# A new written-out order of pieces from the 560th on, and a one-column exponential ahead of softmax exponentials, in a fused attention and token-mixing kernel

## Chip, core and metric

One Trainium2 chip, one of its cores. The metric is device time in microseconds (us). TensorE (PE; its weight loads are PEld), VectorE (DVE), ScalarE (ACT) and GpSimd (POOL) each work through one queue of instructions in order; SyncE (SP) issues the transfers. PE's results stand in PSUM banks, which DVE and ACT read.

## What is computed

Eight batches of 576 tokens. Attention with keys and values pooled by eight, then a token and channel mix with a data-dependent rotation:

```
k_p, v_p = mean of k, v over 8 tokens
attn = softmax(scale * q @ k_p^T) @ v_p               # 8 heads of 64
x = heads side by side                                # 8 x 576 x 512
theta = x @ w_theta
zr, zi = x * cos(theta), x * sin(theta)
u = x + w_tok_r @ zr + w_tok_i @ zi
out = u + max(u @ w_ch, 0)
```

## The kernel before

Matrix products run in three terms (high times high, high times low, low times high) so that each factor is split into a rounded high part and a low rest. The work of a batch `b` is cut into streams, each a Python generator, and each step of a generator up to its `yield` is one piece. The names of the streams are the letters in the schedule:

- `k`, `K`, `Q`, `v`, `V` load and pool keys and values and load queries of a batch.
- `S b.m` (`soften`, one of five tiles of queries): scores on PE (tile `s`, or `s_av` and `s_px`), row maximum (L761), subtraction into `e_eps` (L778), the exponential on ACT (L782), sum, reciprocal (L784, L786), division into `en` (L789, L796), and a transposition into `G`.
- `E` and `X` (`turn`, `attend`): the weights times the values, into the banks `pv_av`, `pv_px`, `pv_s`; copies to `xa` or `xb` follow.
- `Y` and `y` turn `x` through DRAM into `xt`.
- `T b.m` (`rotate`, `theta`): 12 matmuls into the one bank `pt` (L932); ACT rounds it into `g` (L936); DVE subtracts it from `pt` (L938), and with that the bank is free; ACT takes the sine of `g` (L983), ACT or DVE its absolute value (L946, L948), ACT the cosine (L987, a sine with an offset). DVE or POOL multiply both into `z` (L990, L992). The tiles `g` and `sn` have one buffer each.
- `Z b.c` (`take`): a cast of a chunk of `z` into `zh` and the rest into `zl`.
- `M b.c.h` (`mix`): 27 matmuls into a bank `py` of 256 or 320 columns (L1038), DVE adds them to `x` (L1044), and the sum is split into `uh` and `ul`.
- `F b.c.h` (`final`): 12 matmuls into a bank `pf` (L1066), DVE adds the positive part (L1071), transposes (L1077), and four transfers write the output. `py` and `pf` share two banks.

What sets the order is a table of 2131 words. Each word names a stream and runs its next piece; a last letter `v`, `g` or `a` is the engine (DVE, POOL, ACT) for a piece that can be put on several:

```python
    for word in SCHEDULE.split():
        name, engine = (word[:-1], word[-1]) if word[-1] in "vga" else (word, None)
        now[0] = engine
        next(streams[name])
```

So the order of the words is the order of the instructions on each engine. ACT holds one set of function tables at a time: sine and exponential are in different sets, and the compiler puts an ACT_TABLE_LOAD ahead of an activation whose set isn't there. Copies and casts by all engines stand under the helper's line L206 (ACT) or L208 (DVE, POOL), and POOL's arithmetic under L191.

Of the kernel before, what the change touches and what calls it, by code (L numbers as in the profile page):

```python
# [58 lines left out]
F0.2.1 S2.3 Z1.0a M1.1.0 M1.1.1 S2.2 M1.1.1 S2.3 M1.1.1 S2.3 Z1.0g M1.0.1 S2.3g F0.2.0 S2.3v F0.3.1 M1.0.1 S2.4 X2.0
S2.4 M1.1.1 X2.0a S2.3 M1.0.1 S2.4 V3.0g K3 X2.0a Y2.0 S2.4g Y2.0 M1.0.0 S2.4g Y2.0 X2.0a M1.0.1 T2.0a M1.0.0 K3a  # L60
T2.0g F0.1.1 Q3.1 F0.3.1 S2.4 Z1.3a Q3.1 M1.0.0 T2.0 T2.0 Z1.3v M1.0.1a K3 K3a M1.0.1g Y2.0 S3.2 T2.0 Y2.0 Z1.2a V3.2v
T2.0 E2.2 S3.2 T2.1a M1.3.1 M1.1.1g M1.0.0 S3.4 S3.3 Z1.2g y2.0 M1.3.0 S3.2 F0.0.1 M1.3.0 T2.0 T2.0 T2.0a S3.2 M1.1.0a
M1.3.0 E2.2 M1.1.1g M1.3.1 S3.2g S3.2v S3.3 T2.0 M1.3.0 M1.2.1 T2.0g T2.1g S3.3 M1.3.1 v3.1 S3.3 F0.1.1 M1.2.1 T2.1
S3.2 S3.3g S3.3v M1.3.1 M1.3.0a S3.4 k4.2 T2.1 X2.2 M1.3.1g F0.0.1 S3.3 V3.1g S3.4 T2.1 M1.2.0 F0.2.1 M1.2.1 S3.4 Y2.2
X2.2a Y2.2 F0.2.1 Y2.2 M1.2.0 X2.2a M1.0.0a S3.4g k4.0 X2.2a T2.2a Y2.2 T2.0v S3.4v S3.0 S3.4 Y2.2 T2.2g u3 M1.2.1
M1.2.1g T2.1 T2.1 S3.0 S3.1 M1.2.0 T2.1 M1.2.1g M1.3.1v V3v F1.3.1 E3.2 T2.1a T2.1 M1.3.0g F1.3.1 M1.2.0 F1.3.1 T2.1v
S3.0 F1.3.1 F1.1.1 y2.2 M1.2.0g M1.2.0g F1.1.1 F1.1.1 T2.1v T2.3a E3.2 S3.0 S3.0v T2.2 F1.3.1 F1.3.1 F1.1.1 T2.2 T2.2
S3.0g F1.0.1 S3.1 T2.4g T2.2 T2.2 F1.2.1 F1.1.1 F1.0.1 M1.1.0v F1.1.1 T2.3v F1.2.1 K4.0g F1.0.1 M1.0.0g F1.0.1 S3.1
T2.3 S3.0 T2.3 S3.1 F1.2.1 F1.2.1 X3.2 T2.3 T2.2 T2.2a k4.1 F1.2.1 T2.2 T2.2g T2.2g T2.3 F1.0.1 F1.0.0 F1.2.0 K4.2g
S3.1g F1.0.0 X3.2a X3.2a X3.2v T2.3 Y3.2 F1.2.0 T2.4a T2.4a T2.4v T2.3 T2.3a F1.2.1 F1.2.0 T2.4 F1.0.1 T2.4 T2.4 T2.3  # L70
T2.3g F1.0.0 Y3.2 Y3.2 T2.3v T2.4 S3.1g F1.2.0 F1.0.0 Q4.0 T2.4 Y3.2 F1.1.0 T2.4 S3.1 K4.1g F1.1.0 T2.4 T2.4v k5.0
T2.4 F1.1.0 T2.4 F1.1.0 T2.4 K4 Z2.1v F1.3.0 F1.2.0 K4a E3.0 F1.3.0 Z2.1v F1.3.0 E3.0 Z2.0a M2.1.0 F1.3.0 M2.1.0 Q4.0
M2.1.0 Z2.0v M2.1.1 M2.1.0 K5.0v M2.1.1 M2.1.1 M2.1.1 M2.1.1g T3.3a M2.0.0 M2.0.1 T2.4 M2.0.1 F1.2.0 M2.1.0v M2.0.1 K4
Z2.2v T2.4 M2.1.1v v4.1 T3.3v Y3.2 F1.1.0 M2.0.1 F1.1.0 v4.2 M2.0.1v X3.0 M2.0.0 M2.0.0 Z2.3v M2.0.0 F1.0.0 Y3.0
F1.3.0 X3.0v X3.0v X3.0v Q4.1 T3.1v Y3.0 Y3.0 T3.1v Z2.2g V4.1g K4a Z2.3v M2.2.1 M2.3.0 M2.2.1 M2.2.1 T3.1 V4.2g
M2.1.0v k5.2 M2.2.1 T3.1 M2.3.0 T3.1 Q4.1 M2.2.1v M2.2.0 S4.0 K5.2g M2.2.0 T3.1 T3.1 M2.2.1g Y3.0 M2.2.0 T3.0a Y3.0
S4.0 v4.0 M2.0.0g M2.3.0 F1.0.0 y3.0 T3.0g T3.0 S4.0 S4.0 S4.0v S4.0g T3.1 M2.3.0 V4.0g S4.1 S4.0 M2.2.0 v5.2 T3.1a
T3.0 T3.0 M2.3.1 M2.3.1 S4.1 T3.1 T3.1v M2.2.0a S4.1 T3.1g T3.0 S4.1 S4.1v T3.0 Q5.0 T3.2a y3.2 S4.1g S4.1 M2.3.1 T3.0
S4.2 T3.3 M2.3.0v M2.2.0g T3.0a T3.2v T3.0 M2.3.1 T3.0v T3.3 F1.3.0 M2.0.0v F2.2.0 T3.0v F2.0.0 T3.3 T3.3 k5.1 K5.1g
M2.3.1a F2.0.0 V4v M2.3.0v F2.0.0 M2.0.1v T3.3 F2.0.0 S4.2 F2.2.0 T3.3 T3.3a F2.0.0 T3.3 F2.2.0 S4.2 E4.0 E4.0 V5.2g  # L80
F2.2.0 M2.3.1v T3.2 T3.3v F2.1.1 T3.2 F2.0.0 T3.3v T3.2 F2.2.1 F2.1.1 F2.1.1 T3.2 S4.2 T3.2 S4.2g F2.2.1 F2.1.1 F2.2.1
S4.3 S4.2v F2.2.1 T3.2 F2.3.1 v5.1 S4.3 F2.0.1 T3.2a T3.2 T3.2g F2.3.1 u4 T3.2g F2.3.1 S4.4 S4.2 Z3.0a S4.3 Z3.1a
F2.2.1 F2.2.0 F2.0.1 F2.0.1 K5 F2.3.1 F2.0.1 Q5.0 S4.3 k6.2 M3.0.0 S4.3v F2.1.0 F2.1.0 Z3.0g S4.3g V5g F2.1.0 M3.0.0
F2.1.0 F2.2.1 F2.1.0 V5.1g S4.4 M3.0.0 F2.2.0 F2.3.0 Q5.1 F2.3.0 F2.3.0 K5a F2.3.0 F2.3.0 K5 X4.0 M3.0.0 S4.3 F2.3.0
X4.0a Y4.0 v5.0 X4.0a M3.0.1 Y4.0 Z3.1v M3.0.1 M3.0.1 M3.1.1 X4.0a S4.4 S4.4 Y4.0 S4.4v Z3.2a T4.0a S4.4v F2.1.0
M3.0.1 T4.1a T4.0g V5.0g M3.1.1 Q5.1 S4.4 T4.0 M3.1.0 M3.1.1 Y4.0 M3.1.0 M3.1.1 K5a S5.2 Z3.2g Y4.0 S5.2 S5.2 M3.1.0
E4.2 M3.0.0a F2.0.1 E4.2 T4.1v Z3.3a M3.1.0 S5.2 S5.3 y4.0 S5.2g T4.0 M3.2.1 S5.2v T4.0 u5 S5.3 M3.2.1 S5.3 T4.0
F2.3.1 M3.3.0 S5.4 T4.0 S5.3 S5.2 Z3.3g S5.3v T4.0 T4.0a M3.3.0 M3.1.1a M3.0.1v M3.2.1 M3.3.0 T4.1 S5.3v M3.0.1v S5.4
T4.0 F2.0.1 F2.1.1 M3.2.1 v6.1 X4.2 S5.4 T4.1 M3.3.1 T4.0g Q6.0 F2.1.1 S5.4 F2.3.1 M3.2.1v T4.1 M3.3.1 S5.3 T4.0g
X4.2a Y4.2 M3.3.0 M3.1.1v M3.2.0 T4.1 Y4.2 M3.1.0g Y4.2 V6.1g M3.3.0g X4.2v S5.4g Y4.2 S5.4g M3.2.0 T4.1 S5.4 X4.2a  # L90
S5.0 M3.2.0 T4.2v K6.2g S5.0 M3.0.0g M3.1.0v T4.2v T4.1 Y4.2 M3.3.1 M3.3.1 S5.1 T4.3v T4.2 M3.3.1a T4.1v T4.2 F3.1.1
M3.2.0 T4.2 k6.0 E5.2 S5.0 M3.2.1v M3.3.1v T4.3g F3.3.1 y4.2 F3.3.1 F3.1.1 F3.1.1 F3.3.1 S5.0 T4.1 M3.2.0a E5.2 S5.0v
S5.0g T4.1g S5.1 F3.3.1 T4.1g F3.1.1 S5.1 F3.0.1 F3.3.1 F3.1.1 S5.1 T4.2 F3.2.1 M3.3.0g F3.2.1 F3.3.1 K6.0g F3.0.1
F3.1.1 F3.2.1 F3.0.1 F3.2.1 T4.2 T4.2 T4.2a T4.2 T4.3 M3.2.0g S5.0 T4.2v F3.0.1 F3.0.1 T4.4a T4.2v T4.3 T4.3 F3.2.1
X5.2 Y5.2 S5.1g X5.2a F3.0.0 F3.1.0 F3.0.0 X5.2a X5.2v F3.1.0 T4.4v T4.3 S5.1g T4.3 F3.0.0 v6.2 T4.3 T4.3a k6.1 F3.0.1
T4.4g T4.3 T4.4v T4.3g T4.3g Y5.2 S5.1 T4.4 Y5.2 F3.1.0 F3.1.0 F3.0.0 F3.2.1 T4.4 T4.4 K6.1g T4.4 F3.2.0 F3.3.0 F3.3.0
T4.4 F3.3.0 F3.2.0 T4.4 T4.4 F3.2.0 K6 F3.3.0 T4.4v Y5.2 E5.0 T4.4 T4.4 K6a T4.4 K6 E5.0 T5.3a Z4.0v F3.0.0 F3.0.0
M4.0.0 M4.0.0 F3.2.0 Z4.0v Z4.1a v6.0 M4.0.0 M4.0.1 M4.0.0 M4.0.1 M4.1.0 Y5.2 M4.1.0 T4.4 V6.2g T4.4 M4.0.1 Z4.2a
# [10 lines left out]
M5.0.0 M5.0.0 S6.3 F4.1.1 S6.3g S6.3g M5.0.0 F4.1.1 M5.0.1 K7 F4.2.1 S6.4 M5.0.0 S6.4 M5.0.1 F4.3.0 X6.0 M5.0.1 K7a
S6.4 Z5.1v M5.1.0 S6.3 S6.4g F4.2.1 M5.1.0 M5.0.1 F4.0.1 X6.0a M5.1.0 S6.4v F4.0.1 F4.3.0 Y6.0 F4.0.1 S6.4 M5.1.0 Y6.0  # L110
M5.1.1 Z5.2a X6.0v M5.1.1 Q7.1 X6.0v F4.1.1 Y6.0 Q7.1 M5.1.1 F4.0.1 M5.1.1 E6.2 S7.2 S7.2 Z5.3a S7.2 Z5.2g Z5.3v
M5.2.1 M5.2.1 S7.3 E6.2 M5.3.1 S7.2 Y6.0 S7.2g M5.0.0g Y6.0 S7.2g M5.2.1 V7.1g M5.0.1v S7.3 F4.0.1 M5.0.1v M5.3.1 X6.2
# [1094 lines left out]
```

## Time and profile before

| what | value |
|---|---|
| median of 3 runs | 594.06 us (590.54, 594.06, 595.79) |
| the profiled execution | 590.58 us, span of its instructions 588.8 us |
| busy: PE, DVE, POOL, ACT | 559.9, 434.6, 306.8, 291.2 us |
| mean granted clock of PE | 0.986 |

Times inside the profile are counted from the first instruction. In a row of the timeline the bracket at the end is the idle time of the engine before the instruction, and what ended it. PE's busy time takes in the modelled ends of pipelined matmuls, so that it says when PE stood still, and not how fast it ran.

### The profile page before, as it was taken

How to read it: one execution, taken by the hardware profiler on the slowest of the kernel's cores; microseconds unless marked ns; L12 is line 12 of the kernel's file. 1: busy time of each engine (PE TensorE's matmuls, PEld its weight loads, DVE VectorE, ACT ScalarE, POOL GpSimd, SP SyncE). 2: the span in 40 equal slices, each digit the busy share in tenths (PEclk: the TensorE clock that was granted, in tenths of full speed). 3: DMA queues.
4: the chain of work that ended last, by engine and by line, in shares of the span. 5: the costliest groups of instructions: out<-in, count | busy, mean ns of one | idle time of the engine just before them, and what ended most of it. 6: DMA issues, size and time to landing. Idle time of an engine off the chain costs nothing.

```text
span 588.8 us, 13209 instructions
## 1 busy us (share of the span) xinstructions
PE 559.9 (95%) x4904; PEld 500.6 (85%) x4904; DVE 434.6 (74%) x857; ACT 291.2 (49%) x589; POOL 306.8 (52%) x445
## 2 busy tenths in 40 slices
...
GB/s 260 269 281 117 117 86 44 122 130 147 97 125 128 164 128 110 163 182 96 132 114 150 165 124 106 191 147 91 80 103 146 68 48 21 90 90 30 13 49 73
DMA packets 191265, 70.63 MB, mean 120 GB/s; under 512 B 149600, under 2 KB 176224, under 8 KB 191200
## 3 DMA queue, kind: packets, MB, share of 16 engines
...
q8 instruction: 39, 0.64, 0.5%
...
HBM read 45.15 MB, written 15.73 MB: 103 GB/s over the span
## 4 chain that ended last, share of the span: by engine, by line
PE 79%; DVE 7%; DMA 4%; POOL 4%; SPq 2%; issue 2%; ACT 2%; POOLq 0%; DVEq 0%; ACTq 0%
PE py L1038 37%; PE pt L932 15%; PE pf L1066 14%; PE s L719 2%; SPq L848 2%; PE pv_av L879 2%; PE pv_av L870 1%; DMA z<-in_v_dram 1%; PE pv_px L870 1%; PE vpp L598 1%; POOL xl L191 1%; PE warm L298 1%; PE s_av L719 1%; PE kpp L598 1%; DMA kprst<-in_k_dram 1%
## 5 line engine op out<-in xcount | busy, mean ns | idle before, releaser
L1038 PE MATMUL py<-WTh,zh 128*128 128x256 f32 (+1 forms) x576 | 87.1, 298 | 2.1 <-DVE zh L208 2.0
L1038 PE MATMUL py<-WTl,zh 128*128 128x256 f32 (+1 forms) x576 | 87.6, 296 | 0.0
L1038 PE MATMUL py<-WTh,zl 128*128 128x320 f32 (+1 forms) x576 | 85.6, 296 | 0.9 <-DVE xb L1044 0.9
L1038 PEld LDWEIGHTS py<-WTh,zh 128*128 128x128 f32 x576 | 80.4, 190 | 4.9 <-DVE zh L208 2.6
L1038 PEld LDWEIGHTS py<-WTl,zh 128*128 128x128 f32 x576 | 80.4, 189 | 1.2 <-issue 0.8
L1038 PEld LDWEIGHTS py<-WTh,zl 128*128 128x128 f32 x576 | 78.9, 188 | 3.0 <-DVE xb L1044 1.3
L191 POOL TENSOR_TENSOR zl<-z,zh 128x384 fp32r<-128x384 f32 (+1 forms) x68 | 53.6, 821 | 29.3 <-ACT zh L206 18.2
L191 POOL TENSOR_TENSOR en<-e_eps,ri 128x256 f32<-128x256 f32 (+3 forms) x66 | 40.3, 630 | 40.4 <-DVE ri L786 27.7
L936 ACT ACTIVATE g<-pt,c_magic 128x512 f32<-128x512 f32 x35 | 24.1, 688 | 57.8 <-PE pt L932 48.2
L932 PE MATMUL pt<-th,xh 128*128 128x512 f32 x148 | 41.9, 405 | 5.3 <-DVE g L938 5.1
L206 ACT CAST zh<-z 128x1152 fp32r<-128x1152 f32 x22 | 25.4, 1152 | 42.8 <-PE py L1038 38.3
L1066 PE MATMUL pf<-uh,chh 128*128 128x256 f32 (+1 forms) x256 | 43.6, 297 | 1.2 <-DVE xb L1071 1.2
L1066 PE MATMUL pf<-ul,chh 128*128 128x256 f32 (+1 forms) x256 | 44.3, 297 | 0.0
L1066 PE MATMUL pf<-uh,chl 128*128 128x256 f32 (+1 forms) x256 | 43.6, 295 | 0.0
L932 PE MATMUL pt<-tl,xh 128*128 128x512 f32 x148 | 41.5, 403 | 0.0
L932 PE MATMUL pt<-th,xl 128*128 128x512 f32 x148 | 41.0, 400 | 0.0
L1066 PEld LDWEIGHTS pf<-uh,chh 128*128 128x128 f32 x256 | 37.5, 188 | 4.0 <-DVE xb L1071 1.8
L1066 PEld LDWEIGHTS pf<-uh,chl 128*128 128x128 f32 x256 | 37.4, 188 | 1.4 <-issue 0.5
L1066 PEld LDWEIGHTS pf<-ul,chh 128*128 128x128 f32 x256 | 37.4, 188 | 1.0
L782 ACT ACTIVATE e_eps<-e_eps 128x576 f32<-128x576 f32 (+1 forms) x30 | 20.6, 687 | 35.4 <-DVE e_eps L778 35.2
L1044 DVE TENSOR_TENSOR xb<-py,xb 128x320 f32<-128x320 f32 x32 | 15.5, 484 | 26.1 <-PE py L1038 25.7
L932 PEld LDWEIGHTS pt<-th,xh 128*128 128x128 f32 x148 | 25.4, 188 | 10.5 <-issue 2.6
...
## 6 DMA issues: line engine op xcount, KB each, us to landing
...
out_dram<-R SPq DMA_DIRECT2D x112, 40.0 KB
out_dram<-R SPq DMA_DIRECT2D x112, 32.0 KB
```

What stands on the lines that cost most here:

```text
L191: nc.gpsimd.tensor_tensor(out[:, r], a[:, r], b[:, r], op)
L206: nc.scalar.copy(out, src)
L598: nc.tensor.matmul(main[:, 2 * j : 2 * j + 2, :], ident, st[:, :, D * r : D * r + D], **steps[r])
L719: nc.tensor.matmul(scs[hh][o : o + 64, SP * c : SP * c + SP], qT[r, c, t0 + o : t0 + o + 64], kpT[r, c, SP * hh : SP * hh + SP], start=Tru ...
L782: nc.scalar.activation(e[:n], e[:n], AF.Exp, scale=scale)
L848: queue.dma_start(Ex[32 * j : 32 * j + 32, 0:m, i], Gx[32 * i : 32 * i + 32, 0:m, j])
L870: nc.tensor.matmul(out(a, y)[half(x_)], Vs[b][half(y), c], weights(half(y), c), start=True, stop=False,)
L932: nc.tensor.matmul(pt, l[:, c, :], r[:, c, :], start=i == 0, stop=i == 11)
L936: nc.scalar.activation(g, pt, AF.Identity, bias=c_magic)
L1038: nc.tensor.matmul(py[:, :n], l[:, kk, :], r[:, kw, t], start=i == 0, stop=i == 3 * NK - 1)
L1044: nc.vector.tensor_tensor(u, py[:, :n], u, ALU.add)
L1066: nc.tensor.matmul(pv[:, :n], l[:, kk, o], uhl[r][:, kk, t], start=i == 0, stop=i == 11)
```

## The change

Counted from 0, words 0 to 559 of the table stay. From the 560th on (while batch 0 is mixed, near 110 us of the profile) the same 1571 pieces stand in another order: a piece moves by 8 places in the mean, the farthest by 131. 149 of them run on another engine: 44 go from DVE to POOL, 33 from POOL to DVE, 27 from DVE to ACT, 17 from ACT to POOL, 16 from POOL to ACT, 12 from ACT to DVE. Counted over the built program, ACT has 39 instructions more (566 for 527), DVE 29 fewer (830 for 859), POOL 11 more; PE and SP have the same instructions in another order. Table loads on ACT are 44 instead of 40. An exponential stands between the sine and the cosine of one `T` piece, with a load before each, five times instead of three times.

The second part is in `soften` and `rotate`: where the last activation was a sine, a one-column exponential of a constant is issued ahead of the softmax exponential, 20 times in all. It waits for nothing, so that the load that the compiler puts before it waits for nothing either.

```diff
+    c_one = const([P, 1], F32, "c_one")
...
+    table = [None]
+    def exp_table():
+        if table[0] != AF.Exp:
+            nc.scalar.activation(c_one, c_eps, AF.Exp)
+            table[0] = AF.Exp
+    def sine(*args, **kw):
+        nc.scalar.activation(*args, AF.Sin, **kw)
+        table[0] = AF.Sin
...
+            exp_table()
             nc.scalar.activation(e[:n], e[:n], AF.Exp, scale=scale)
...
-            nc.scalar.activation(s, g, AF.Sin, scale=-TWO_PI)
+            sine(s, g, scale=-TWO_PI)
...
-M0.0.1a T1.1a k3.0 T1.4 F0.0.0 K3.0g F0.1.0 T1.1 F0.0.1 S2.0 T1.1 T1.1 T1.4 S2.1 F0.2.0 F0.0.0 S2.1 T1.4 Q3.0 T1.4
+M0.0.1a T1.1a k3.0 T1.4 F0.0.0 K3.0g F0.1.0 T1.1 F0.0.1 S2.0 T1.4 T1.3g T1.1 T1.1 F0.0.0 S2.1 T1.4 S2.1 T1.4 F0.2.0
...
```

The added lines move the line numbers by 13 in `soften` (L719 becomes L732) and by 15 from there on (L1038 becomes L1053), and all sines stand under L707, all one-column exponentials under L703.

Place 1, near 254 to 262 us, tiles of batches 2, 3 and 4. PE before, the rows right behind the scores `s4_1`, up to the third theta of batch 3, `pt3_3`:

```order
L932 MATMUL pt3_0_3449<-tl_107,xh3_0_3420 128x512 x4
L932 MATMUL pt3_0_3449<-th_106,xl3_0_3421 128x512 x4
L1038 MATMUL py2_3_1_3500<-WTh_516,zl2_3_3254 128x320 x9
L1038 MATMUL py2_3_1_3500<-WTl_517,zh2_3_3253 128x320 x9
L1038 MATMUL py2_3_1_3500<-WTh_516,zh2_3_3253 128x320 x9
L719 MATMUL s4_2_3566<-kpT_101,qT4_2981 64x72 x16
L932 MATMUL pt3_3_3583<-th_106,xh3_3_3144 128x512 x4
```

PE after, from the same scores to the same theta:

```order
L1053 MATMUL py2_3_0_3307<-WTh_517,zl2_3_3261 128x256 x9
L1053 MATMUL py2_2_0_3383<-WTl_518,zh2_2_3186 128x256 x9
L947 MATMUL pt3_0_3492<-th_107,xh3_0_3376 128x512 x4
L947 MATMUL pt3_0_3492<-tl_108,xh3_0_3376 128x512 x4
L1053 MATMUL py2_2_0_3383<-WTh_517,zl2_2_3187 128x256 x9
L732 MATMUL s4_2_3525<-kpT_102,qT4_2956 64x72 x16
L947 MATMUL pt3_0_3492<-th_107,xl3_0_3377 128x512 x4
L1053 MATMUL py2_3_1_3549<-WTh_517,zl2_3_3261 128x320 x9
L1053 MATMUL py2_3_1_3549<-WTl_518,zh2_3_3260 128x320 x9
L1053 MATMUL py2_3_1_3549<-WTh_517,zh2_3_3260 128x320 x9
L1081 MATMUL pf2_0_0_3590<-uh2_3209,chh_962 128x256 x4
L947 MATMUL pt3_3_3613<-th_107,xh3_3_3173 128x512 x4
```

The scores move ahead of three sets of nine mix matmuls and of the first four matmuls of `pt3_0`. ACT in the same place before, from the cosine of batch 3's tile 1 to the rounding of tile 0:

```order
L987 ACTIVATE g3_1_3404<-g3_1_3404,c_cos_96 128x512
L206 CAST uh2_3141<-xa2_2190 128x256
L782 ACT_TABLE_LOAD
L782 ACTIVATE e_eps_103<-e_eps_103 128x8x72
L936 ACTIVATE g3_0_3531<-pt3_0_3449,c_magic_92 128x512
```

ACT after, between the same two:

```order
L707 ACTIVATE g3_1_3432<-g3_1_3432,c_cos_97 128x512
L206 CAST xh3_2_3518<-xb3_2867 128x512
L703 ACT_TABLE_LOAD
L703 ACTIVATE c_one_95<-c_eps_94 128x1
L797 ACTIVATE e_eps_104<-e_eps_104 128x8x72
L206 CAST uh2_3209<-xa2_2222 128x256 x2
L951 ACTIVATE g3_0_3595<-pt3_0_3492,c_magic_92 128x512
```

The load now belongs to the one-column exponential; two casts stand between the softmax exponential and the rounding.

Place 2, near 473 to 479 us: DVE behind the attention product of batch 7 (`pv7_256`), up to the subtraction that frees the bank of `pt6_1`. Before:

```order
L902 STREAM_TRANSPOSE xs7_2_6417<-pv7_256_av_6398 128x8x32
L902 STREAM_TRANSPOSE xs7_2_6417<-pv7_256_px_6399 128x8x32
L902 STREAM_TRANSPOSE xs7_2_6417<-pv7_256_s_6400 128x8x32 x2
L208 COPY xb7_6397<-pv7_256_s_6400 128x640
L208 COPY xe6_6087<-xb7_6397 128x4x64
L208 CAST xh7_2_6455<-xb7_6397 128x512
L789 TENSOR_TENSOR en7_0_6462<-e_eps_103,ri7_0_6253 128x2x4x64
L938 SCALAR_TENSOR_TENSOR g6_1_6430<-g6_1_6430,pt6_1_6361 128x512
```

After:

```order
L917 STREAM_TRANSPOSE xs7_2_6398<-pv7_256_av_6374 128x8x32
L1086 SCALAR_TENSOR_TENSOR xb5_4662<-pf5_0_1_6304,xb5_4662 128x320
L1092 STREAM_TRANSPOSE R5_3_1_6406<-xb5_4662 128x320
L917 STREAM_TRANSPOSE xs7_2_6398<-pv7_256_px_6375 128x8x32
L1092 STREAM_TRANSPOSE R5_0_1_6424<-xb5_4662 128x320
L208 COPY xb7_6373<-pv7_256_s_6376 128x640
L917 STREAM_TRANSPOSE xs7_2_6398<-pv7_256_s_6376 128x8x32 x2
L953 SCALAR_TENSOR_TENSOR g6_1_6467<-g6_1_6467,pt6_1_6393 128x512
```

The copy to `xe6`, the cast of `xh7_2` and the division `en7_0` no longer stand ahead of the subtraction; on PE the product `pv7_256` now comes before `pt6_1`, and 24 `pf` matmuls of 256 columns stand between `pt6_1` and `pt6_4`.

Place 3, near 218 to 222 us: the cast of batch 2's first chunk, `zh2_1`, on which the first mix of batch 2 waits. DVE before:

```order
L948 TENSOR_SCALAR g2_4_2976<-g2_4_2976 128x512
L1005 TENSOR_TENSOR z_108<-px2_4_3000,sn2_4_3014 64x512
L1071 SCALAR_TENSOR_TENSOR xa1_1373<-pf1_1_0_2995,xa1_1373 128x256
L1007 TENSOR_TENSOR z_108<-px2_4_3000,g2_4_2976 64x512
L208 CAST zh2_1_3032<-z_108 128x1152
```

ACT after:

```order
L961 ACTIVATE g2_4_2985<-g2_4_2985 128x512
L707 ACTIVATE g2_4_2985<-g2_4_2985,c_cos_97 128x512
L206 COPY kpT_102<-pk4_3013 64x4x72
L206 COPY kpT_102<-pk4_3013 64x3x72
L206 COPY kpT_102<-pk4_3013 64x8
L206 CAST zh2_1_3048<-z_109 128x1152
```

Absolute value and cast have moved from DVE to ACT, the cast behind three copies of the keys.

## Rows read from the trace of the kernel before

**Rows 1.** Page, part 1: busy time, share, instructions of each engine.

```profile
PE 559.9 (95%) x4904; PEld 500.6 (85%) x4904; DVE 434.6 (74%) x857; ACT 291.2 (49%) x589; POOL 306.8 (52%) x445
```

**Rows 2.** Stretches: busy time and count of PE, PEld, DVE, ACT, POOL, then PE's clock.

```profile
110.00:588.80 478.80, 462.21 (x4081) 417.14 (x4079) 343.47 (x679) 209.23 (x326) 263.85 (x379) 0.99 0.50 109
476.00:479.60 3.60, 1.63 (x31) 1.29 (x20) 3.50 (x8) 0.87 (x3) 0.64 (x1) 1.00 0.60 146
479.70:483.00 3.30, 3.30 (x10) 2.51 (x9) 3.25 (x8) 1.23 (x2) 0.62 (x1) 0.50 0.00 0
...
580.00:600.00 20.00, 2.27 (x20) 2.06 (x18) 2.13 (x5) 0.00 (x0) 0.00 (x0) 0.87 0.16 26
```

**Rows 3.** PE's waits from 110 us on: total, times, longest.

```profile
PE pt L932 <- DVE g L938: 5.1, 5, 2.0
PE py L1038 <- DVE zh L208: 1.3, 2, 1.0
PE pf L1066 <- DVE xb L1071: 1.2, 2, 0.6
PE pkr L620 <- ACT kpT L206: 0.9, 1, 0.9
PE py L1038 <- DVE xb L1044: 0.9, 1, 0.9
```

**Rows 4.** Timeline, 254 to 262.5 us: start, length, engine, instruction.

```profile
254.04 0.23 PE L719 MATMUL s_px<-kpT,qT 64*64 64x72 f32 x2
...
258.03 1.28 ACT L782 ACT_TABLE_LOAD   x1 [1.09 <-DVE e_eps L778]
...
259.32 0.69 ACT L782 ACTIVATE e_eps<-e_eps 128x576 f32<-128x576 f32 x1
...
261.68 0.68 DVE L938 SCALAR_TENSOR_TENSOR g<-g,pt 128x512 f32<-128x512 f32 x1
...
262.42 1.19 PE L932 MATMUL pt<-th,xh 128*128 128x512 f32 x4 [1.48 <-DVE g L938]
```

**Rows 5.** Chain of work that ended last: start, length, what; one term each.

```profile
522.32 1.06 PE py L1038 x9
...
528.48 0.93 PE pt L932 x4
```

**Rows 6.** Timeline, 454 to 480 us.

```profile
454.10 1.28 ACT L782 ACT_TABLE_LOAD   x1 [1.92 <-DVE e_eps L778]
...
461.54 1.17 PE L932 MATMUL pt<-th,xh 128*128 128x512 f32 x4 [0.83 <-DVE g L938]
...
466.88 0.74 PE L1066 MATMUL pf<-uh,chh 128*128 128x256 f32 x4 [0.58 <-DVE xb L1071]
...
477.17 1.10 DVE L789 TENSOR_TENSOR en<-e_eps,ri 128x512 f32<-128x512 f32 x1
478.19 0.68 DVE L938 SCALAR_TENSOR_TENSOR g<-g,pt 128x512 f32<-128x512 f32 x1
...
479.02 1.49 PE L932 MATMUL pt<-th,xh 128*128 128x512 f32 x4 [1.97 <-DVE g L938]
```

**Rows 7.** Timeline, 221 to 222.5 us.

```profile
221.39 1.16 ACT L206 CAST zh<-z 128x1152 fp32r<-128x1152 f32 x1 [0.35 <-DVE z L1007]
221.39 0.76 DVE L208 CAST zh<-z 128x1152 fp32r<-128x1152 f32 x1
...
222.21 1.33 PE L1038 MATMUL py<-WTh,zh 128*128 128x256 f32 x9 [1.01 <-DVE zh L208]
```

**Rows 8.** Timeline: another wait of PE, 367 us.

```profile
367.16 1.00 PE L1038 MATMUL py<-WTh,zl 128*128 128x320 f32 x5 [0.85 <-DVE xb L1044]
```

**Rows 9.** ACT's groups: busy, mean ns, idle before, what ended it.

```profile
L782 ACT ACT_TABLE_LOAD x18 | 23.1, 1283 | 7.7 <-DVE e_eps L778 7.5
L936 ACT ACTIVATE g<-pt,c_magic 128x512 f32<-128x512 f32 x35 | 24.1, 688 | 57.8 <-PE pt L932 48.2 <-POOL z L191 3.6 <-DVE z L992 3.3
L766 ACT ACTIVATE mx<-mx 128x8 f32<-128x8 f32 (+1 forms) x10 | 2.0, 203 | 3.9 <-DVE mx L761 3.7
```

More of the change, by code (lines that the diff above doesn't have):

```diff
@@ L59 @@
[L59 to L98, printed above, removed]
@@ L109 @@
[L109 to L112, printed above, removed]
-F4.1.1 S7.2 S7.3 M5.2.1 S7.3 M5.1.1a X6.2a X6.2v M5.3.0 Y6.2 M5.3.0 M5.2.1a Y6.2 M5.3.1 S7.3g Y6.2 S7.3v u7 X6.2a S7.4
@@ new lines @@
+k6.2 T4.0g M3.1.1 S5.3 Y4.0 S5.2 T4.1v V5.0g Y4.0 Z3.2v M3.1.1 S5.2 F2.1.1 Z3.2g E4.2 T4.0 T4.0 M3.1.0 y4.0 S5.2
+M3.1.0 S5.2 M3.1.1 T4.0 E4.2 Z3.3a M3.1.0 M3.2.1 S5.2v M3.0.1a T4.0 T4.0 S5.2g M3.1.0 F2.3.1 S5.3 M3.2.1 T4.0 S5.3
+Z3.3g S5.4 M3.0.0a M3.3.0 T4.1 M3.2.1 T4.0v v6.1 S5.3 M3.0.1v S5.2 M3.3.0 F2.1.1 M3.1.1g S5.3v T4.1 S5.3g M3.3.0 T4.0
+M3.2.1 T4.0g T4.1 S5.4 u5 S5.4 T4.0g F2.0.1 X4.2 M3.3.1 M3.2.1a V6.1g M3.3.0 S5.3 Y4.2 X4.2a Y4.2 Y4.2 X4.2a V5g X4.2a
+S5.4 T4.2v S5.0 S5.4g M3.3.1 S5.4g T4.1 T4.3a Q6.0 S5.0 M3.3.1 M3.2.0 S5.4 T4.1 Y4.2 M3.2.0 M3.2.0 M3.2.1g M3.3.1
```

120 lines of the change are left out of this document (80 added, 40 removed).

## The prediction, made before the changed kernel was run

> **What bounds the kernel now.** I read the page's busy times first: PE is busy 559.9 us of a span of 588.8 [rows 1], so a gain can come only from time in which PE stands or runs slowly. The stretches split that: from 110 us on, where the order changes, PE is busy 462.21 of 478.80 us [rows 2], which leaves 16.6 us. Then the view of PE's own waits in that stretch, by whom it waited for: 5.1 for the subtraction that frees the theta bank, 1.3 for the cast of the mix's first operand, 1.2 and 0.9 for the DVE additions that free a `py` or `pf` bank or make `x`, 0.9 for key copies [rows 3]; together 9.4 us. Most of the other 7 us is the end of the program, which no order shortens: in the last 8.8 us PE is busy 2.27 [rows 2], and then DVE and the output transfers are left. The clock view adds one thing: between 479.7 and 483 us PE ran at 0.50 of its clock, the lower of its two levels, right after a stretch in which it was busy 1.63 of 3.60 us [rows 2]. Those 3.3 us did the work of half as long, so 1.7 us were lost. **All that a better order can win is about 9.4 + 1.7 = 11.1 us**, 1.9% of the profiled 590.58.
>
> The timeline tells what made PE wait, and twice it is ACT. Near 258 us the softmax exponential needs its table; the load starts at 258.03, when DVE's subtraction ends, takes 1.28, the exponential follows at 259.32, and behind it in ACT's queue stands the rounding of a theta. The DVE step that frees the bank therefore runs at 261.68, and PE, ready 1.48 us before, goes on at 262.42 [rows 4]. Near 454 the load again starts only after the wait, and the chain through sine and cosine ends in 0.83 us of waiting at 461.54 [rows 6]. The group of ACT's loads shows how often this is so: the 18 loads ahead of a softmax exponential stood 7.5 us in all for the subtraction, the loads alone [rows 9].
>
> **The one-column exponential.** Its load waits for nothing, so that 1.28 us go from behind the wait to ahead of it wherever the load waited. A one-column activation isn't in the trace; the nearest row, eight columns, takes 0.203 us [rows 9], and nothing reads its result, so 0 to 0.2 each, 20 of them, 4.1 us of ACT at most. ACT is idle some 300 us of the span [rows 1] and stood 57.8 us ahead of the theta rounding alone, 48.2 of it for PE [rows 9]. That cover hides it; without it, it costs the 4.1. The four extra loads (44 for 40) are 4 x 1.283 = 5.1 us of ACT under the same cover, and they come from thetas with an exponential between sine and cosine, which hold the only `g` buffer longer.
>
> On that the rows show the load at 258.03 with 1.28, the activation at 259.32 [rows 4]: 1.29 for a switch, no more. The Trainium skill's page "ScalarE: Activation LUTs", section "What ACT_TABLE_LOAD costs", gives about 1.28 for the load and 1.38 for a drain, some 2.66 us for every switch, and its section on table sets asks to batch calls by set, which speaks against this change; by it the four loads would be an estimated 10.6 us of ACT and not 5.1. The trace shows no such drain, so the sum goes by the row.
>
> **Place 1, 262 us.** Before, 8.1 us pass from the end of the scores `s4_1` (254.27) to the theta that waited (262.42) [rows 4]; the PE work between them is 8.1 - 1.5 = 6.6. After, that work grows by three sets of nine 256-column matmuls at 1.06 and one set of four theta matmuls at 0.93 [rows 5], and four `pf` matmuls (4/9 of 1.06, 0.5): 6.6 + 3.2 + 0.9 + 0.5 = 11.2 us. The chain loses the 1.28 of the load, and gains two casts on ACT and one more multiplication on DVE, at most 0.7 each by the row of DVE's step at 261.68: 8.1 - 1.3 + 2.1 = 8.9. So 2.3 us of cover are left and the 1.48 us go.
>
> **Place 2, 454 to 484 us.** Here 0.83 + 0.58 + 1.97 us of waits and the 1.7 us of slow clock lie [rows 2, 6], 5.1 in all. The longest, 1.97 at 479.02, is a queue on DVE: the subtraction that frees the bank stands behind copies and a division of 1.10 [rows 6]. In the new order those three are elsewhere, and PE has `pv7_256` ahead of `pt6_1` and 24 `pf` matmuls (24/9 of 1.06 = 2.8 us) behind it, against a rounding of 0.69 and a subtraction of 0.68: covered by more than a microsecond. The 0.58 was a `pf` group that started right behind the one whose bank it takes; in the new order no group in this stretch does. The 0.83 falls with the load, of 1.28. I leave 0.5 us there for queues that I can't see, and take the slow clock as gone, since PE has no hole of that size left to bring it on. Gain 4.6; 0 if the waits only move.
>
> **Place 3, 222 us.** PE waits 1.01 us for the cast `zh`, which took 0.76 on DVE; the same cast on ACT took 1.16 [rows 7]. It goes to ACT, behind three key copies, but the absolute value leaves DVE's queue as well, and one DVE addition is no longer ahead of the last multiplication. Between 0.5 less and 0.9 more; I take no change.
>
> **The rest of the 11.1** is 9.4 - 1.5 - 3.4 - 1.0 = 3.5 us of waits at some seven places, the longest of them 0.9 each, for key copies [rows 3] and, at 367.16, for an addition on DVE [rows 8]. I can't follow each of them in the new order: half goes, 1.7; bounds 0 and 3.5.
>
> **New waits.** 1571 pieces move, and places that fit by a few tenths will miss. The bounds are 0 and 9.4, what the order before pays in the same stretch. I take 2.5, a quarter, nearer to 0, because in the whole new order, from 110 us on, I count one group of `py` or `pf` that follows the one whose bank it takes by only four matmuls (0.6 us), and in the order before two such and one that follows at once.
>
> **The engines' loads.** DVE loses 29 instructions of 434.6/857 = 0.51 us, 15 us; ACT gains the 9.2 above and some 15 others of 291.2/589 = 0.49, together 17; POOL 11 of 0.69, 8 [rows 1]. DVE, the busiest after PE, gets lighter and the others have room, so nothing is counted for it.
>
> **Sum.** -1.5 (place 1) - 4.6 (place 2) + 0 - 1.7 + 2.5 = -5.3 us, so 590.58 - 5.3 = 585.3 for an execution like the profiled one. The three runs were 590.54, 594.06 and 595.79, and with the profiled one half the executions stand near 590.5 and half near 595. Their middle is 592.3, and the median that will be measured is as likely to come from one half as from the other: 592.3 - 5.3 = **587 us**, 1.2% under the median shown.
>
> **Rivals.** (a) *The waits only move* (0.33): the places above are cured, and as many new ones open, since the new order packs PE as tightly and DVE still does 420 us of work in one queue. For it speaks that nearly all of PE's waits are DVE's queue [rows 3] and not a missing resource; against it, that the two longest have a cause that the order names. The time is then 592.3, and between 590.5 and 594 by the half of the runs. (b) *The longer hold of `g` reaches PE* (0.1), slower. Two more thetas, one of batch 2 and one of batch 4, have an exponential between sine and cosine: each holds `g` and `sn` by two loads, the small and the full exponential longer, 2.57 + 0.2 + 0.69 = 3.5 us. Thetas of a batch follow each other through that one buffer, and the first mix of the batch waits for the last of them; at batch 2 it waits already (place 3). If nothing hides it, 7 us, and with all of ACT's 17 us in the chain up to 17. It decides from the point where ACT no longer stands idle before the rounding; 57.8 us of such idleness [rows 9] speak against it. With 12 in the middle: 592.3 + 12 - 5.3 = 599. By the 2.66 us for a switch in the Trainium skill ("ScalarE: Activation LUTs", "What ACT_TABLE_LOAD costs") the four extra loads would put an estimated 5.5 us more on it, 604; the rows show no drain. (c) *The new exponential does nothing* (0.07): the 18 loads stood only 7.5 us in all for the subtraction [rows 9], so most ran ahead of it anyway, and where one didn't the compiler may still keep it behind. Then place 1 is still covered by the order (8.9 + 1.3 = 10.2 against 11.2), place 2 loses 0.8, and the time is 588.
>
> **Chances.** The forecast has 0.5. A difference of 1%, about 6 us, is what a measurement of this kernel can tell from none. Faster by more than that, under 588.1: three quarters of the forecast (0.38) and the luckier part of (a) and (c) (0.12), 0.50. Within 1%: the rest of the forecast (0.12) and most of (a) and (c) (0.27), 0.39. Slower: (b) and the worst of (a), 0.11. The range goes from 580 (no new waits, all 11.1 gone: 592.3 - 11.1 = 581, or 579.5 from a run near 590.5) to 596, the waits moved in a run of the slower half; (b) lies beyond.
>
> **What the changed profile would show.** PE's waits from 110 us on near 5 us instead of 9.4. No idle bracket at the theta behind `s4_1`; all loads ahead of a softmax exponential back to back with the instruction before them. PE's clock at its upper level near 480 us. At the first mix of batch 2 about 1 us still. Wrong would be a sum of waits of 9 or more with other names; a wait of the first mixes for casts that grew by 3 us would be (b).

## The result and the profile after

| kernel | median, us | runs | lowest to highest | ratio to before, 95% interval |
|---|---|---|---|---|
| before | 593.5 | 20 | 590.54 to 596.16 | |
| changed | 588.48 | 20 | 586.5 to 591.96 | 0.9916, 0.990 to 0.9932 |

The change gains 5.0 us, 0.84%; the forecast was 5.3 less and 587. The execution of the changed kernel that was profiled took 590.8 us, span 589.0, the third slowest of its 20. The profile before was of one of the fastest, 590.58. So the two spans are equal although the medians are 5 us apart, and a comparison has to start where the order changes.

The timeline of the kernel before shows a transfer in the common beginning, an attention product near the first moved word, and the last matmuls; then the view of stretches between the last two.

```profile
32.03 4.21 PE L598 MATMUL vpp<-z,ident 128*128 128x128 f32 x21 [0.37 <-DMA z<-in_v_dram]
...
108.59 0.37 PE L879 MATMUL pv_av<-xt,Vr 32*64 32x256 f32 x1
...
581.64 0.63 PE L1066 MATMUL pf<-ul,chh 128*128 128x256 f32 x4
```

```profile
108.60:582.20 473.60, 463.54 (x4103) 418.20 (x4087) 343.93 (x679) 210.16 (x328) 263.85 (x379) 1.00 0.50 110
```

The same two views of the changed kernel, and four stretches that answer to [rows 2].

```profile
35.11 1.19 PE L599 MATMUL vpp<-z,ident 128*128 128x128 f32 x4 [3.88 <-DMA z<-in_v_dram]
...
112.88 0.37 PE L894 MATMUL pv_av<-xt,Vr 32*64 32x256 f32 x1
...
581.51 0.63 PE L1081 MATMUL pf<-ul,chh 128*128 128x256 f32 x4
```

```profile
112.90:582.10 469.20, 462.26 (x4103) 418.63 (x4087) 332.06 (x650) 225.34 (x367) 269.65 (x390) 0.99 0.53 111
...
110.00:589.00 479.00, 465.20 (x4132) 420.79 (x4130) 334.08 (x656) 226.26 (x370) 270.71 (x392) 0.99 0.54 111
253.40:260.20 6.80, 5.94 (x16) 4.79 (x17) 2.40 (x3) 1.81 (x4) 1.43 (x3) 0.50 0.95 203
476.00:479.60 3.60, 3.60 (x29) 3.40 (x28) 3.23 (x7) 2.08 (x4) 1.33 (x4) 1.00 0.25 52
479.70:483.00 3.30, 3.30 (x46) 2.52 (x45) 3.17 (x8) 1.45 (x3) 1.42 (x2) 1.00 0.75 136
```

The unmoved beginning took 4.3 us longer in this execution (112.88 against 108.59), most of it at one load of values for which PE stood 3.88 us instead of 0.37. From there to the last matmul the changed kernel needs 469.20 us instead of 473.60: 4.4 less, near the 5.0 of the medians. The same rows split the 4.4. PE stands 6.94 us instead of 10.06: 3.1 less. The slow clock costs half of 5.94, 3.0 us, instead of half of 3.30, 1.65 [rows 2]: 1.3 more. What is left is PE's work at full clock, 459.3 instead of 461.9: 2.6 less for the same 4103 matmuls, which the forecast had no term for.

PE's waits after, from 110 us on (total, times, longest), and the timeline at the longest of them.

```profile
PE pt L947 <- ACT xh L206: 4.3, 3, 3.0
...
PE py L1053 <- ACT zh L206: 0.3, 1, 0.3
...
PE pf L1081 <- DVE xb L1086: 0.2, 1, 0.2
```

```profile
245.03 0.45 DVE L917 STREAM_TRANSPOSE xs<-pv_av 128x256 f32<-128x256 f32 x1 [0.84 <-PE pv_s L894]
246.95 0.45 DVE L1092 STREAM_TRANSPOSE R<-xa 128x256 f32<-128x256 f32 x1 [1.47 <-DMA out_dram<-R]
...
249.31 1.42 DVE L1038 TENSOR_TENSOR zl<-z,zh 128x640 fp32r<-128x640 f32 x2
250.65 0.44 DVE L917 STREAM_TRANSPOSE xs<-pv_px 128x256 f32<-128x256 f32 x1
251.19 0.75 DVE L521 TENSOR_TENSOR vprst<-vprst 128x256 f32<-128x256 f32 x2
...
253.59 0.62 ACT L206 CAST xh<-xa 128x512 fp32r<-128x512 f32 x1
...
254.26 2.08 PE L947 MATMUL pt<-th,xh 128*128 128x512 f32 x4 [3.01 <-ACT xh L206]
```

Of the names of [rows 3] the mix's wait for `zh` is left with 0.3 and one for a `pf` bank with 0.2: of the 9.4 us of before all but 0.5 are gone. In their place stands one that was not there, 3.01 us up to 254.26 for `xh` of batch 3's tile 1, and from 253.4 us on the clock is at 0.50 for 6.8 us. DVE's queue shows why: between the first and the last transposes of the attention's output stand a wait of 1.47 for an output transfer, the rest `zl` and the pooling of values. The theta behind place 1 starts without a bracket (273.53 below), and the loads have lost their wait, as ACT's groups show.

```profile
262.01 0.23 PE L732 MATMUL s_px<-kpT,qT 64*64 64x72 f32 x2
...
267.96 1.28 ACT L703 ACT_TABLE_LOAD   x1
...
269.25 0.20 ACT L703 ACTIVATE c_one<-c_eps 128x1 f32<-128x1 f32 x1
...
269.36 0.67 ACT L797 ACTIVATE e_eps<-e_eps 128x576 f32<-128x576 f32 x1
...
271.71 0.68 DVE L953 SCALAR_TENSOR_TENSOR g<-g,pt 128x512 f32<-128x512 f32 x1
...
273.53 1.09 PE L947 MATMUL pt<-th,xh 128*128 128x512 f32 x4
```

```profile
L703 ACT ACT_TABLE_LOAD x20 | 25.7, 1283 | 0.3
L951 ACT ACTIVATE g<-pt,c_magic 128x512 f32<-128x512 f32 x35 | 24.0, 686 | 26.0 <-PE pt L947 17.2 <-DVE z L1007 4.5 <-POOL z L191 2.2
```

The 20 loads stood 0.3 us in all, where 18 stood 7.7 [rows 9]. At place 1 itself the load was not early: it starts at 267.96, behind a cosine and a cast in ACT's queue, and DVE's subtraction had ended at 267.63. The small exponential won nothing there. And ACT's idle time ahead of the theta rounding, in which I saw the cover, has fallen from 57.8 to 26.0.

### The profile page after: what moved, and what is told of

It reads as the page before. It is cut to its first block, busy times and chain, and to the rows that moved or that the text cites. A ratio compares the mean times of both kernels' runs of the same rounds, so it can differ in the third digit from the quotient of the medians.

```text
span 589.0 us, 13253 instructions
## 1 busy us (share of the span) xinstructions
PE 559.2 (95%) x4904; PEld 501.9 (85%) x4904; DVE 423.4 (72%) x828; ACT 306.6 (52%) x628; POOL 313.2 (53%) x456
## 4 chain that ended last, share of the span: by engine, by line
PE 67%; DMA 10%; SPq 8%; DVE 6%; POOL 4%; issue 2%; ACT 2%; DVEq 0%; POOLq 0%; ACTq 0%
PE py L1053 30%; PE pf L1081 13%; PE pt L947 13%; SPq L1097 3%; SPq L863 3%; DMA kpst<-in_k_dram 3%; PE s L732 2%; DMA out_dram<-R 2%; DMA z<-in_v_dram 2%; DMA kprst<-in_k_dram 1%; PE pv_av L885 1%; PE pv_av L894 1%; PE vpp L599 1%; POOL xl L191 1%; DMA xt<-hall 1%
## 5 line engine op out<-in xcount | busy, mean ns | idle before, releaser
L1053 PE MATMUL py<-WTh,zh 128*128 128x256 f32 (+1 forms) x576 | 87.2, 299 | 0.9 <-DVE zh L208 0.6
L1053 PE MATMUL py<-WTl,zh 128*128 128x256 f32 (+1 forms) x576 | 87.9, 297 | 0.0
L1053 PE MATMUL py<-WTh,zl 128*128 128x320 f32 (+1 forms) x576 | 86.6, 298 | 0.0
L1053 PEld LDWEIGHTS py<-WTh,zh 128*128 128x128 f32 x576 | 80.7, 191 | 4.0 <-issue 1.6
L1053 PEld LDWEIGHTS py<-WTh,zl 128*128 128x128 f32 x576 | 80.0, 190 | 2.8 <-issue 1.3
L1053 PEld LDWEIGHTS py<-WTl,zh 128*128 128x128 f32 x576 | 80.6, 190 | 0.7 <-issue 0.4
L191 POOL TENSOR_TENSOR z<-xt,sn 128x256 f32<-128x256 f32 x30 | 22.5, 771 | 21.2 <-ACT sn L707 15.9
```

The source lines that it names most:

```text
L191: nc.gpsimd.tensor_tensor(out[:, r], a[:, r], b[:, r], op)
L1053: nc.tensor.matmul(py[:, :n], l[:, kk, :], r[:, kw, t], start=i == 0, stop=i == 3 * NK - 1)
```

## The experiments

Each is compared with the kernel before, run on the same chip (593.6 to 594.3 us).

**The one-column exponential, left out and alone.**

```diff
-        if table[0] != AF.Exp:
+        if False:
```

> The changed kernel with the one-column exponential left out (new order and new engines stay). The theory: the order covers the waits, and the load ahead of the softmax exponential is worth 0 to 1.5 us, so 588.5 to 590, a ratio to the kernel before of 0.992 to 0.994. The rival, that the early load is the gain: 592 to 593.5, a ratio of 0.998 to 1.0. In the profile the loads ahead of the softmax exponential again wait for the subtraction, about 7 us in all, and the wait of 3.0 us for the cast xh near 251 us, which starts long before the softmax that follows, stands as it did.

Measured: 587.58, ratio 0.9896 (0.9872 to 0.992), no slower than with it. The loads at the softmax wait again, 5.9 us in all, and place 1 stays free of a wait. So order and engines bring the whole gain. The wait for `xh` did not stay at 3.0, as I had expected: it is 2.15 us in this profile, and no slow clock follows it.

```diff
+            exp_table()
             nc.scalar.activation(e[:n], e[:n], AF.Exp, scale=scale)
```

> The kernel before with the one-column exponential added and nothing else. The theory: the waits of PE at 262 us (1.48) and 461 us (0.83) lose up to 1.28 and 0.83, together at most 2.1 us, and nothing else moves: 591.4 to 593.5, a ratio of 0.996 to 1.0. The rival, that the early load is the gain: about 588.5, a ratio of 0.992.

Measured: 592.34, ratio 0.9982 (0.9965 to 0.9999): at most 2 us, as the theory had it. Place 1 in its timeline:

```profile
264.10 0.69 ACT L951 ACTIVATE g<-pt,c_magic 128x512 f32<-128x512 f32 x1 [2.10 <-POOL z L191]
...
265.56 1.20 PE L947 MATMUL pt<-th,xh 128*128 128x512 f32 x4 [0.72 <-DVE g L953]
```

The load is out of the way, and the wait falls only from 1.48 to 0.72, not by 1.28: now the rounding stands 2.10 us for POOL's last product with the theta before, which holds the one `g`. The next thing was 0.5 us behind the load. And the longest wait of PE in this profile is a new one, 20 us on:

```profile
282.26 0.85 DVE L819 STREAM_TRANSPOSE G<-en 128x640 f32<-128x640 f32 x1 [1.65 <-DMA eraw<-G]
...
284.93 0.45 DVE L1092 STREAM_TRANSPOSE R<-xa 128x256 f32<-128x256 f32 x1 [1.43 <-DMA out_dram<-R]
...
285.89 1.30 PE L1053 MATMUL py<-WTh,zh 128*128 128x256 f32 x9 [2.21 <-ACT e_eps L797]
```

The bracket names ACT's exponential, but on DVE the addition that empties a bank of `pf` stands right behind these two transposes, from 285.29 on, and ends near 285.8; so the wait is more likely DVE's, for two transfers. In the kernel before only the second of them was waited for, 1.34 us, and PE did not wait. In this execution, the slowest of twelve, more was lost there than place 1 had won.

**Order and engines, apart.** All pieces in the new order on their old engines, and the reverse; no one-column exponential.

```diff
-F0.2.0 S2.4g Y2.0 S2.4 T2.0g T2.0g M1.0.1 Z1.2a T2.0 T2.0 K3 K3a Q3.1 Y2.0 Z1.3v V3.2g M1.0.1v S3.2 T2.0 T2.1a S3.2
+F0.2.0 S2.4g Y2.0 S2.4 T2.0a T2.0g M1.0.1 Z1.2a T2.0 T2.0 K3 K3a Q3.1 Y2.0 Z1.3v V3.2v M1.0.1a S3.2 T2.0 T2.1a S3.2
```

> The new order with every piece on the engine that it had before, and without the one-column exponential. If the order of PE's work is what covers the waits: 588.5 to 591, a ratio of 0.992 to 0.996. The rival, that the order needs the other engines (DVE has 15 us more to do, and PE waits for DVE most): 593 or more, a ratio of 0.999 to 1.01.

Measured: 596.49, ratio 1.0049 (1.0027 to 1.0071). PE's longest waits are for DVE, the engine that the letters had made lighter:

```profile
PE pf L1081 <- DVE xa L1086: 2.7, 1, 2.7
PE py L1053 <- DVE zl L1038: 2.4, 1, 2.4
```

```diff
-S2.4 M1.1.1 X2.0a S2.3 M1.0.1 S2.4 V3.0g K3 X2.0a Y2.0 S2.4g Y2.0 M1.0.0 S2.4g Y2.0 X2.0a M1.0.1 T2.0a M1.0.0 K3a
+S2.4 M1.1.1 X2.0a S2.3 M1.0.1 S2.4 V3.0g K3 X2.0a Y2.0 S2.4g Y2.0 M1.0.0 S2.4g Y2.0 X2.0a M1.0.1 T2.0g M1.0.0 K3a
```

> The order before, with the 149 pieces on their new engines and without the one-column exponential. The theory, by which a lighter DVE by itself is worth nothing: 592.5 to 595, a ratio of 0.998 to 1.003. The rival, that PE's waits are DVE's load: 589 to 591, a ratio of 0.993 to 0.996. A third case: pieces put on engines that are busy at their old place make new waits, 596 or more.

Measured: 611.39, ratio 1.0304 (1.0276 to 1.0333). PE's longest wait is one of 7.1 us for the rest `ul`; POOL's timeline there:

```profile
271.69 2.20 POOL L191 TENSOR_TENSOR kpst<-kpst 128x256 f32<-128x256 f32 x3 [6.49 <-DMA kpst<-in_k_dram]
...
275.32 0.72 POOL L191 TENSOR_TENSOR ul<-xa,uh 128x256 fp32r<-128x256 f32 x1
```

The order alone costs 2.8 us, the engines alone 17.7, both together gain 6.1 (the run without the exponential). That is no sum: what a new engine is worth depends on what stands ahead in that engine's queue. Here a rest `ul` that PE needs stands on POOL behind the pooling of keys, which waits 6.49 us for its load.

**Where the gain lies.** The table is cut at a word, and behind it the pieces not yet used follow in the other table's order. The first diff is against the changed kernel, the next two against the kernel before, whose one-column exponential they also have.

```diff
-F2.0.1 F2.0.1 F2.0.1 Q5.0 F2.2.0 S4.3 F2.1.0 F2.2.1 Z3.0g S4.3 S4.3g F2.1.0 M3.0.0 F2.1.0 u4 S4.3v V5.1g K5a Z3.1g
+F2.0.1 F2.0.1 u4 S4.3 F2.0.1 Q5.0 S4.3 k6.2 M3.0.0 S4.3v F2.1.0 F2.1.0 Z3.0g S4.3g V5g F2.1.0 M3.0.0 F2.1.0 F2.2.1
...
```

> The new order up to word 1099 (about 290 us) and behind it the remaining pieces in the order and on the engines of before; one-column exponential in both parts. By the two profiles the new order has lost some 5 us against the old one by then (a wait of 3.0 us for xh and the slow clock behind it), so the theory that the gain lies in the second half says 597 to 600, a ratio of 1.006 to 1.011. If the lost 5 us are only of the one execution that was profiled: 590 to 592, a ratio of 0.994 to 0.998. A bad seam would show as waits near 290 us.

Measured: 597.93, ratio 1.0053 (1.0028 to 1.0078).

```profile
PE pt L947 <- DVE g L953: 2.8, 3, 2.0
PE pt L947 <- ACT xh L206: 2.6, 1, 2.6
```

```diff
-F2.2.1 F2.2.0 F2.0.1 F2.0.1 K5 F2.3.1 F2.0.1 Q5.0 S4.3 k6.2 M3.0.0 S4.3v F2.1.0 F2.1.0 Z3.0g S4.3g V5g F2.1.0 M3.0.0
+F2.2.1 F2.2.0 F2.0.1 F2.0.1 K5 F2.3.1 F2.0.1 Q5.0 F2.2.0 F2.1.0 F2.2.1 Z3.0g S4.3 S4.3g F2.1.0 M3.0.0 F2.1.0 S4.3v
...
```

> The order of before up to word 1099, and behind it the remaining pieces in the new order and on the new engines; one-column exponential in both parts. If the gain lies in the second half (place 2 at 454 to 484 us and the small waits from 330 us on): 583 to 588, a ratio of 0.983 to 0.991, faster than the whole new order. If both halves gain alike: 590 to 591. If an order is worth something only with the history that it was made for: over 593.

Measured: 583.99, ratio 0.982 (0.9793 to 0.9846), faster than the whole change, and the best version of this study. Its longest waits from 110 us on:

```profile
PE pt L947 <- ACT xh L206: 2.2, 2, 1.2
PE py L1053 <- DVE zh L208: 1.0, 1, 1.0
```

The new first half costs 3.7 us, the second gains 10.3; their sum, 6.6, is near the whole (5.0). Both figures hold the one-column exponential in the part with the old order too, where by itself it gained 1.4. The first half brings its wait for `xh` (2.6) with it, and place 2 as it was (2.0) stays behind the cut. With the cut further back:

```diff
-M5.1.1 Z5.2a X6.0v M5.1.1 Q7.1 X6.0v F4.1.1 Y6.0 Q7.1 M5.1.1 F4.0.1 M5.1.1 E6.2 S7.2 S7.2 Z5.3a S7.2 Z5.2g Z5.3v
+M5.1.1 Z5.2a X6.0v M5.1.1 Q7.1 X6.0v F4.1.1 Q7.1 V7.1g Y6.0 Z5.2g M5.1.1 Z5.3a F4.0.1 E6.2 F4.0.1 M5.1.1 S7.2 E6.2
...
```

> The order of before up to word 1639 (about 425 us), the new order and engines behind it, one-column exponential in both parts. If place 2 (waits of 0.83, 0.58 and 1.97 us and 1.7 us of slow clock) is the core of the second half's gain of 10 us: minus 4 to 6, 588 to 590, a ratio of 0.990 to 0.993. If that gain is spread over the stretch from 290 us on: minus 2 to 3, 591 to 592. If the first part of the second half brings it all: 593 to 594.

Measured: 587.08, ratio 0.9886 (0.9862 to 0.9909), 6.5 us less, a little more than expected. Of the 10.3, some 6.5 lie behind 425 us, and 3.8 between 290 and 425. Less the 1.4 of the exponential in the old order, the 6.5 are about the 5.1 that place 2 held; this subtraction is an estimate.

**The best order without the exponential.** The new second half, with `if False:` as above.

> The order of before up to word 1099, the new order and engines behind it, and no one-column exponential in either part. If ACT's time is not free (the 59 us of more loads cost 36), the 19 small activations, 3.9 us, cost up to 2.3 and the early loads win up to 1: 582 to 585. If the early load is the gain: 588 or more. If neither matters: 584, as with it.

Measured: 587.11, ratio 0.989 (0.9865 to 0.9916), slower than 583.99 with it, and between the figures expected. Place 1, which is in the old order here, waits 1.58 us, with the exponential 0.58. But in the view of stretches, from the attention product near 110 us to the last matmul, the two profiled executions need the same; the first row is with the exponential, the second without.

```profile
109.10:575.60 466.50, 459.84 (x4103) 416.64 (x4087) 341.45 (x671) 220.49 (x356) 256.17 (x374) 1.00 0.53 112
...
112.40:578.50 466.10, 459.59 (x4103) 416.24 (x4087) 341.97 (x671) 218.06 (x337) 256.84 (x374) 1.00 0.53 112
```

Their spans, 581.1 and 584.3, differ by the unmoved beginning, 109.1 against 112.4 us, which has no one-column exponential in either. So that the early load is worth 3.1 us in this order stands on the medians alone, six runs each on two chips; the traces show one wait that is 1.0 shorter and no time won by it.

**The wait for `xh`: output transfers on ACT.** Twice, with the two groups of batch 1 at two places in ACT's queue.

```diff
-            (nc.scalar if b == B - 1 and i % 2 else nc.sync if b == B - 1 else queue).dma_start(
+            on_act = (b, c, hf) in ((1, 1, 0), (1, 2, 0), (3, 0, 0), (3, 2, 0))
+            (nc.scalar if b == B - 1 and i % 2 or on_act else nc.sync if b == B - 1 else queue).dma_start(
```

The words of these pieces move with them; those lines are left out here.

> The changed kernel with four groups of output transfers (of the final pieces 1.1.0, 1.2.0, 3.0.0 and 3.2.0) issued by ACT, which stands idle there, instead of SP, whose queue they stood in behind the sixteen reads of G; the two of batch 1 right behind their transpose. The theory, that the new waits for xh at 254 and 381 us (3.0 and 0.9 us) come from SP's queue by way of DVE's transposes into R (idle 1.47 and 2.95 us for the earlier transfers): DVE's waits there go, PE's waits become 0.5 to 1.6 and 0 to 0.3, the time falls by 2 to 5 us to 583.5 to 586.5, a ratio of 0.983 to 0.988. The rival, that the pooled values and the copies in DVE's queue hold xh anyway: the waits stay above 2.5 and the time is 588 to 589.

Measured: 591.56, ratio 0.9939 (0.9913 to 0.9966), above all that was expected. DVE's wait of 1.47 is gone and `xh` is waited for 0.97 us, but the transfers now stand in ACT's queue ahead of the cast that the first mix needs:

```profile
228.76 0.58 PE L1053 MATMUL py<-WTh,zh 128*128 128x256 f32 x1 [2.53 <-ACT zh L206]
```

> The kernel with four groups of output transfers on ACT once more, but the two of batch 1 now stand in ACT's queue behind the cast of the mix's first operand and the last copy of the keys, so that nothing waited for stands behind them for 12 us. If the theory of SP's queue holds: the wait of 2.5 us for the cast zh near 229 us and the slow clock behind it go, the wait for xh near 254 us stays at about 1, and the time is 583 to 586.5, a ratio of 0.982 to 0.988. The rival, that shortening this one wait is given back at the next: 588 to 590, a ratio of 0.990 to 0.993.

Measured: 589.12, ratio 0.9926 (0.9905 to 0.9947): the rival's figure. The first mix waits 1.27, `xh` still 1.90. The Trainium skill, page "DMA: Bandwidth & Descriptors", section "Rules for kernel authors", says that spreading transfers over SP and ACT gives no bandwidth and only saves time in issuing; here even the saved issuing bought nothing.

**The wait for `xh`: DVE's queue.**

```diff
-F1.3.0 M2.1.0v M2.3.0 M2.0.0a F1.0.0 M2.1.0v v4.2 X3.0a M2.0.1v Z2.3v X3.0a Y3.0 V4.2v Y3.0 X3.0a M2.3.0 V4g T3.1a
+F1.3.0 M2.1.0v M2.3.0 M2.0.0a F1.0.0 M2.1.0v v4.2 X3.0a M2.0.1v X3.0a Y3.0 Y3.0 X3.0a Z2.3v V4.2v M2.3.0 V4g T3.1a
```

> The changed kernel with two words moved behind the last copy of the attention's output: the rest zl of chunk 3 of batch 2 and the pooling of values that stood in DVE's queue between the transposes of that output. If the new wait for xh near 254 us is DVE's queue (2.4 us of those two pieces, besides the transposes into R): the wait falls from 3.0 to 0.6 us or less, the slow clock behind it goes, and the time is 582.5 to 586.5, a ratio of 0.981 to 0.988. The rival, that what is won there is given back at the next place, as with the transfers on ACT: 588 to 589.5, a ratio of 0.990 to 0.993.

Measured: 588.73, ratio 0.992 (0.9893 to 0.9948): the time of the changed kernel. Its timeline at the theta, and 29 us later:

```profile
245.39 0.73 DVE L917 STREAM_TRANSPOSE xs<-pv_s 128x256 f32<-128x256 f32 x2
...
248.35 1.09 PE L947 MATMUL pt<-th,xh 128*128 128x512 f32 x4
...
273.71 2.72 POOL L191 TENSOR_TENSOR kpst<-kpst 128x256 f32<-128x256 f32 x3 [9.68 <-DMA kpst<-in_k_dram]
...
277.34 0.41 PE L611 MATMUL pk<-ident,kp 128*64 128x128 f32 x2 [2.14 <-POOL kp L191]
```

The cause was right: the theta starts without a wait, and the slow clock behind it is gone. The gain was not: PE reaches the transposes of the keys earlier, the keys' load does not come earlier, and PE stands 2.14 us there. The pooling of these keys starts at 273.71, in the profile of the changed kernel at 273.91, although this execution is 3.6 us ahead of that one at the first moved word. From there to the last matmul PE stands 8.0 us (6.9 in the changed kernel). The wait moved.

**ACT's cover.**

```diff
-            nc.scalar.activation(c_one, c_eps, AF.Exp)
+            for f in (AF.Exp, AF.Sin, AF.Exp):
+                nc.scalar.activation(c_one, c_eps, f)
```

> The changed kernel with the one-column exponential replaced, at each of its 20 places, by three one-column activations (exponential, sine, exponential), so 40 more loads of 1.28 us and 40 more small activations of 0.2: 59 us more of ACT. If ACT's idle time covers table loads, as the prediction took it: plus 0 to 4 us, 588.5 to 592.5. If a load is paid in full: plus 59. If each is paid where a theta or a cast stands behind it on ACT, about a third: plus 15 to 25, 603 to 613. A load that also drained the engine for longer than its own time would show as idle time in the rows behind it.

Measured: 624.31, ratio 1.0493 (1.0463 to 1.0524): 35.8 us more than the changed kernel for 59 of ACT, between the second and the third case. Timeline of one of its places:

```profile
302.41 1.28 ACT L704 ACT_TABLE_LOAD   x1
303.70 0.20 ACT L704 ACTIVATE c_one<-c_eps 128x1 f32<-128x1 f32 x1
...
306.84 0.67 ACT L798 ACTIVATE e_eps<-e_eps 128x576 f32<-128x576 f32 x1
...
307.54 0.76 DVE L800 TENSOR_REDUCE sm<-e_eps 128x8 f32<-128x584 f32 x1 [3.24 <-ACT e_eps L798]
...
308.78 0.42 DVE L1087 SCALAR_TENSOR_TENSOR xa<-pf,xa 128x256 f32<-128x256 f32 x1
...
309.26 1.01 PE L1082 MATMUL pf<-uh,chh 128*128 128x256 f32 x3 [3.24 <-DVE xa L1087]
```

ACT delays the exponential, DVE stands for it in its queue for 3.24 us, the addition behind it frees a bank that late, and PE stands the same 3.24. So ACT, idle half the time, passes on 0.6 us of each that is added at these 20 places, in the mean. A switch of tables takes 1.28 and the activation starts 0.01 later; the drain of 1.38 us of the Trainium skill ("ScalarE: Activation LUTs", "What ACT_TABLE_LOAD costs") does not show here, as it did not in the prediction's rows.

## Why the prediction was right, and where it was not

The direction, the size (5.3 forecast, 5.0 measured) and the main place were right. By its terms:

- **Place 1** (-1.5): right. The wait is gone with and without the one-column exponential, so the order's cover does it. The PE work between the scores and the theta was 11.3 us (262.24 to 273.53), as counted; the chain took 10.2 (to 272.39) and not 8.9, so 1.1 us of cover were left instead of 2.3. In the old order the exponential alone takes 0.76 of the wait and not 1.28, since POOL's product holds `g`.
- **Place 2** (-4.6): right, 5.1. No bracket between 455 and 492 us, PE busy 3.60 of 3.60 in the stretch ahead of the old slow clock, and the clock at its upper level behind it. The order from 425 us on gains 6.5 together with the one-column exponential.
- **Place 3** (0): right. The wait of 1.01 [rows 7] is 0.30 in the profile after, a little below the bound of 0.5 less, and 1.1 to 1.4 in three others of that order (without the exponential, with later transfers on ACT, with two words moved).
- **The rest** (-1.7): of the 3.5 all but some tenths went, twice what was forecast.
- **New waits** (+2.5): the term that was mis-sized. PE's waits after sum to 6.9 us, and the new slow clock takes 3.0: 9.9 us, above the upper bound of 9.4, which had no slow clock in it. I counted only groups that follow too closely the one whose bank they take. The wait that came is of another kind, an operand that travels from PE through DVE's queue and ACT to PE; nothing in the count looked at that.
- **No term at all**: PE's own work at full clock, 2.6 us less for the same matmuls. This and the rest make up for the new waits, so the sum was met partly by luck.
- **ACT's load at nothing**: not a thing to count on; when 59 us were added, 0.6 of each us was paid. Of the change's own 9.2 us, the small exponentials, 4.1, cost nothing that can be measured in this order (588.48 with, 587.58 without). What the four extra loads cost no run here shows by itself.
- **Rival (a)**, that the waits only move, held in the first half, which costs 3.7 us; there the forecast's picture was wrong. **Rival (b)** named the wrong object: the added time of ACT can reach PE, but in the place shown by way of DVE's queue and not by `g`. **Rival (c)**: the loads do run ahead; it is the gain from it that is small.
- **The median**: taking 592.3 as the middle was low; 20 runs gave 593.5, and 593.5 - 5.3 would have been 588.2.

What stays open: why the first half gives back whatever is won at one wait. The profiles offer the transfers: the new wait in the run with the exponential alone and the one in the run with two words moved both stand behind transfers that came no earlier, and the last section shows how tightly they are issued. But relieving SP of four groups did not help, so that is argued and not shown.
